# Float64 weights turned into float32: products on two engines, or moved bits and an int32 add on GpSimd, in another order of the first two units

## The chip, the cores and the metric

The kernel runs on one core of a Trainium2 chip. The core has five engines with a queue of instructions each: TensorE (PE in the profile, its weight loads PEld), VectorE (DVE), ScalarE (ACT), GpSimd (POOL) and SyncE (SP, which here issues transfers). The metric is the device time of one execution in microseconds.

## The reference

A gated linear attention over 768 steps, for 4 batches and 8 heads of 48 channels, and on its output a block of normalization and a two-layer MLP with a residual sum. `w_ch1` is 384 x 1536 and `w_ch2` 1536 x 384; both reach the kernel as float64, the other inputs as float32.

```python
f = 1.0 / (1.0 + np.exp(-f_logit))
for t in range(S):
    state = f[:, :, t, :, None] * state + np.einsum('bhd,bhe->bhde', k[:, :, t], v[:, :, t])
    y[:, :, t] = np.einsum('bhd,bhde->bhe', q[:, :, t], state)
x = y.transpose(0, 2, 1, 3).reshape(B, S, H * D)
mu, var = np.mean(x, -1, keepdims=True), np.var(x, -1, keepdims=True)
xn = (x - mu) / np.sqrt(var + 1e-06) * g_ln
out = x + np.maximum(xn @ w_ch1, 0.0) @ w_ch2
```

## The kernel before

The 768 steps are cut into twelve units of 64 steps of all four batches. A unit has an attention, written as a generator with stages, and an MLP with twelve parts. Each engine executes its instructions in the order in which the program writes them; that order is written out by hand at the end of the kernel (the calls of `do.attention`, `do.mlp` and `weights`), so an instruction that waits holds everything written behind it on its engine.

The stages of a unit's attention, with the tiles and lines that matter here:

- gates: PE transposes the raw `f` (L509), ACT makes the sigmoid `gates` (L542)
- after, upto: DVE's two scans over 1040 columns (L523, L535)
- k, q: PE transposes `k` and `q`, DVE multiplies them out of PSUM into `kh` and `qh` (L559); at the end of q DVE makes `kept`, the decayed state (L568)
- scores: PE multiplies the carried state (L579) and `ps` (L589)
- causal, kt, values: DVE masks the scores into `sc` (L593), PE transposes `kh` (L602), ACT copies that; PE makes `py` (L611), ACT copies it into `x` (L622)
- stats: DVE's statistics of `x` (L626, L627), and on GpSimd `rstd` by an add (L628) and a power (L629), both of two columns
- state: PE makes `pn` (L637), from which the new `state` is made (L642; by ACT in unit 0)
- norm, turn: DVE makes `xn` (L656); PE transposes it into `xp` (L666), and six products on ACT, each of which reads the tile `gain`, make `xt` (L668)

An MLP's first six parts make `ph` with w1 (L681: twelve matmuls as the profile counts them; one relu on ACT, L683). Its last six make `po` with w2 (L688: eight matmuls each, three parts for each half of the unit).

The weights come in twelve pieces of 128 x 768 numbers, six of w1 and then six of w2. Piece i of w1 is all that part i of `ph` needs, and piece i of w2 serves two of the twelve steps of a `po` sum, so that the third part of `po` is the first to need pieces five and six. `fetch` issues the transfer of the next piece from SP into `words`, of which there are three buffers. `split` and `join` make float32 of a piece: `split` (L464 to L472) takes exponent and fraction apart on DVE and turns each into a float32 factor on ACT, `join` (L481 to L485) adds the low word, puts in the sign and multiplies, on DVE. In the profile, names of pieces are cut to their columns (`w_0words` to `w_1280words` for w1, and `w_0` again for each piece of w2).

Unit 0's attention runs first, then unit 0's `ph` parts between unit 1's attention stages, each part behind its piece of w1; then unit 1's `ph` parts, beside which w2's pieces are made; then the `po` parts of units 0 and 1 beside unit 2's attention. From unit 2 on, each unit's MLP runs beside the next unit's attention. `load` issues a unit's four inputs, four transfers of 96 KB for each, from SP; unit 1's `f` is issued between the second and third piece, `gain` behind it.

Of the kernel before, what the change touches and what calls it, by code (L numbers as in the profile page):

```python
# [8 lines left out]
FP32 = mybir.dt.float32  # L9
I32 = mybir.dt.int32  # L10
U32 = mybir.dt.uint32
AF = mybir.ActivationFunctionType
ALU = mybir.AluOpType
# [290 lines left out]
def kernel(  # L304
# [19 lines left out]
    nc = tc.nc  # L324
    B, H, S, D = q.shape
    P = 128
# [12 lines left out]
    EPS = 1e-6  # L339
    LEAST = 1e-12  # L340
    PIECE = 768
    BIAS = 1023 - 127

    outer = ctx.enter_context(tc.tile_pool(name="outer", bufs=1))
    ident = outer.tile([P, P], FP32)
# [7 lines left out]
    consts = fast.enter_context(tc.tile_pool(name="consts", bufs=1))  # L353
    raws = fast.enter_context(tc.tile_pool(name="raws", bufs=3))
    stage = fast.enter_context(tc.tile_pool(name="stage", bufs=3))
# [22 lines left out]
    def load(n, name, engines=(nc.sync,)):  # L378
        if n >= NU:
            return  # L380
        if name == "v":
            vt = raws.tile([P, G, H, D], FP32, tag="rawv", name=f"v{n}")
            loaded[n, name] = vt
        else:
            loaded[n, name] = wide_heads[name, n % 2]
        src = {"f": f_logit, "k": k, "q": q, "v": v}[name]
        for b in range(B):
            engines[b % len(engines)].dma_start(  # L388
                out=loaded[n, name][(b % 2) * T:(b % 2 + 1) * T, b // 2, :, 0:D],
                in_=src[b, :, n * T:(n + 1) * T, :].rearrange("h p d -> p h d"))  # L390
# [15 lines left out]
    for b in range(2):  # L406
        nc.gpsimd.affine_select(out=causal[b * T:(b + 1) * T], in_=causal[b * T:(b + 1) * T],
                                compare_op=ALU.is_ge, fill=0.0, base=0, pattern=[[1, T]],
                                channel_multiplier=-1)
    bias = consts.tile([P, 1], FP32)  # L410
    nc.vector.memset(bias, float(-BIAS))
    full = consts.tile([P, 1], FP32)
    nc.vector.memset(full, 255.0)

    ends = consts.tile([P, NS, E1], FP32)
    nc.vector.memset(ends, 0.0)
# [1 line left out]
    starts, gates = [], []  # L418
# [8 lines left out]
    nc.vector.memset(least, 1.0)  # L427
    state = consts.tile([P, 2, GA, D], FP32)


    def pieces(dst, src, name, by_rows):
        rows, cols = dst.shape[1], dst.shape[2]
        sv = src.rearrange("(c p) f -> p c f", p=P)
        r, w = (PIECE // cols, cols) if by_rows else (rows, PIECE // rows)
        return [(f"{name}{i}_{j}", sv[:, i:i + r, j:j + w], dst[:, i:i + r, j:j + w], r, w)
                for i in range(0, rows, r) for j in range(0, cols, w)]
# [3 lines left out]
    fetched, opened = [], []  # L440

    def fetch():
        if not queue:
            return
        name, src, to, r, w = queue.pop(0)
        if not wide:
            nc.sync.dma_start(out=to, in_=src)
            return
        words = stage.tile([P, r, 2 * w], I32, tag="words", name=f"{name}words")
        nc.sync.dma_start(out=words, in_=src.bitcast(I32))  # L450
        fetched.append((name, words, to, r, w))

    def split():

        if not fetched:
            return
        name, words, to, r, w = fetched.pop(0)
        scale = stage.tile([P, r, w], I32, tag="scale", bufs=2, name=f"{name}scale")
        frac = stage.tile([P, r, w], FP32, tag="frac", bufs=2, name=f"{name}frac")
        wv = words.rearrange("p r (f two) -> p two r f", two=2)  # L460
        low, high = wv[:, 0].bitcast(U32), wv[:, 1]


        nc.vector.tensor_scalar(out=scale, in0=high, scalar1=20, scalar2=0x7FF,  # L464
                                op0=ALU.logical_shift_right, op1=ALU.bitwise_and)
        nc.vector.tensor_scalar(out=frac.bitcast(I32), in0=high, scalar1=0xFFFFF, scalar2=None,
                                op0=ALU.bitwise_and)
        nc.scalar.activation(out=frac, in_=frac.bitcast(I32), func=AF.Copy, bias=1.0,
                             scale=2.0 ** -20)
        nc.scalar.activation(out=scale, in_=scale, func=AF.Relu, bias=bias, scale=1.0)  # L470
        nc.scalar.activation(out=scale, in_=scale, func=AF.Relu, bias=full, scale=-1.0)  # L471
        nc.scalar.activation(out=scale, in_=scale, func=AF.Copy, bias=float(255 << 23),  # L472
                             scale=float(-(1 << 23)))
        opened.append((low, high, scale, frac, to))

    def join():

        if not opened:
            return
        low, high, scale, frac, to = opened.pop(0)  # L480
        nc.vector.scalar_tensor_tensor(out=frac, in0=low, scalar=2.0 ** -52, in1=frac,  # L481
                                       op0=ALU.mult, op1=ALU.add)
        nc.vector.scalar_tensor_tensor(out=scale, in0=high, scalar=-(1 << 31), in1=scale,  # L483
                                       op0=ALU.bitwise_and, op1=ALU.bitwise_or)
        nc.vector.tensor_tensor(out=to, in0=frac, in1=scale.bitcast(FP32), op=ALU.mult)  # L485

# [229 lines left out]

    do = Order()


    fetch()
    fetch()
    load(1, "f")
    nc.sync.dma_start(out=gain, in_=moe_g_ln.rearrange("(c p) -> p c", p=P))
    fetch()
    for name in "kqv":
        load(1, name)

    def weights(*steps):  # L730
        for step in steps:
            step()
            if step is join:
                fetch()

    do.attention(0, "gates", "after", "upto", "k", "q", "scores")
    weights(split)
    do.attention(0, "causal", "kt", "values")
    weights(join, split)
    do.attention(0, "stats", "state")  # L740
    do.attention(1, "gates")
    weights(join, split)
    do.attention(0, "norm", "turn")
    do.mlp(0)
    weights(join, split)
    do.mlp(0)
    for _ in range(3):
        weights(join, split)
        do.mlp(0)
    do.attention(1, "after", "upto", "k", "q")  # L750
    weights(join)
    do.mlp(0)
    do.attention(1, "scores")
    weights(split)
    do.attention(1, "causal", "kt", "values")
    weights(join, split)
    do.attention(1, "stats", "state")
    weights(join)
    do.attention(1, "norm", "turn")
    for part in range(6):  # L760
        do.mlp(1)
        weights(split, join)
        if part == 3:
            for name in "fkqv":
                load(2, name)
    assert not (queue or fetched or opened)
# [20 lines left out]
    for m in range(2, NU):  # L787
        n = m + 1
        for part in range(12):
# [19 lines left out]
            if n == NU and part == 2:  # L809
                worst = consts.tile([P, 1], FP32)  # L810
                nc.vector.tensor_reduce(out=worst, in_=least, axis=mybir.AxisListType.X,
                                        op=ALU.min)
# [6 lines left out]
                                        op0=ALU.is_lt)  # L819
# [36 lines left out]
```

## Time and profile before

| what | us |
|---|---|
| median of 3 runs | 546.14 (545.92 to 546.4) |
| the profiled execution | 545.63, of which its span 543.9 |
| PE busy in the span | 500.2 (92%) |
| PEld, DVE, ACT, POOL busy | 384.9, 212.1, 140.0, 16.4 |

The profile is of one execution; times in it run from the start of the span. Busy time of PE is no measure of its speed, since matmuls are pipelined. Where a row names a wait, it gives the idle time of the engine ahead of the instruction and what ended it.

### The profile page before, as it was taken

How to read it: one execution, taken by the hardware profiler on the slowest of the kernel's cores; microseconds unless marked ns; L12 is line 12 of the kernel's file. 1: busy time of each engine (PE TensorE's matmuls, PEld its weight loads, DVE VectorE, ACT ScalarE, POOL GpSimd, SP SyncE). 2: the span in 40 equal slices, each digit the busy share in tenths (PEclk: the TensorE clock that was granted, in tenths of full speed). 3: DMA queues.
4: the chain of work that ended last, by engine and by line, in shares of the span. 5: the costliest groups of instructions: out<-in, count | busy, mean ns of one | idle time of the engine just before them, and what ended most of it. 6: DMA issues, size and time to landing. Idle time of an engine off the chain costs nothing.

```text
span 543.9 us, 10888 instructions
## 1 busy us (share of the span) xinstructions
PE 500.2 (92%) x4841; PEld 384.9 (71%) x4841; DVE 212.1 (39%) x312; ACT 140.0 (26%) x267; POOL 16.4 (3%) x41
## 2 busy tenths in 40 slices
PE   4556468999999999999999999999999999999995
PEld 3545356767787786786786786786786786786873
DVE  7656883672253243243243243243242342341000
ACT  1656464601221221211211211211221220220210
POOL 3100000000000000000000000000000000000000
PEclk9969787999999999999999999999999999999999
DMA  7973138134150240340340240340330340000001
GB/s 137 230 214 116 58 118 155 20 75 88 39 93 2 57 90 2 60 86 2 63 85 1 60 88 6 67 75 10 65 74 13 63 72 16 16 1 16 16 2 33
DMA packets 109702, 33.82 MB, mean 62 GB/s; under 512 B 102736, under 2 KB 105808, under 8 KB 109648
## 3 DMA queue, kind: packets, MB, share of 16 engines
q1 hardware_dynamic: 108592, 32.85, 29.0%
q8 instruction: 40, 0.66, 0.5%
q10 hardware_dynamic: 1056, 0.20, 0.2%
q14 instruction: 14, 0.11, 0.1%
HBM read 28.31 MB, written 4.72 MB: 61 GB/s over the span
## 4 chain that ended last, share of the span: by engine, by line
PE 84%; DVE 6%; ACT 5%; SPq 2%; DMA 1%; issue 1%
PE po L688 35%; PE ph L681 33%; PE tr L509 5%; PE py L611 4%; PE py L579 2%; PE kp L602 2%; PE ps L589 2%; SPq L388 2%; PE pn L637 2%; DVE w L485 1%; PE xp L666 1%; DMA w_0words<-in_moe_w_ch_dram 1%; DVE w_0scale L483 1%; ACT w_0scale L471 1%; ACT w_0scale L472 0%
## 5 line engine op out<-in xcount | busy, mean ns | idle before, releaser
L681 PE MATMUL ph<-xt,w 128*128 128x256 f32 x864 | 200.9, 389 | 7.8 <-DVE w L485 4.6
L688 PE MATMUL po<-w,h 128*128 128x384 f32 x576 | 192.6, 488 | 0.0
L681 PEld LDWEIGHTS ph<-xt,w 128*128 128x128 f32 x864 | 166.7, 196 | 34.2 <-issue 4.1
L688 PEld LDWEIGHTS po<-w,h 128*128 128x128 f32 x576 | 106.8, 190 | 67.7
L683 ACT ACTIVATE h<-ph 128x512 f32<-128x512 f32 x72 | 42.7, 596 | 168.5 <-PE ph L681 168.5
L693 DVE TENSOR_TENSOR o<-x,po 128x384 f32<-128x384 f32 x24 | 13.3, 553 | 105.2 <-PE po L688 105.2
L523 DVE TENSOR_TENSOR_SCAN after<-gates,ends 128x1040 f32<-128x1040 f32 (+1 forms) x13 | 28.0, 2156 | 35.4 <-ACT gates L542 35.4
L668 ACT ACTIVATE xt<-xp,gain 128x128 f32<-128x128 f32 x72 | 19.9, 376 | 83.1 <-PE xp L666 83.1
L626 DVE BATCH_NORM_STATS2 stats<-x 128x6 f32<-128x384 f32 x24 | 13.0, 543 | 69.0 <-ACT x L622 69.0
L593 DVE TENSOR_TENSOR sc<-ps,causal 128x1024 f32<-128x1024 f32 x12 | 14.7, 1224 | 53.9 <-PE ps L589 53.9
L535 DVE TENSOR_TENSOR_SCAN upto<-gates,starts 128x1040 f32<-128x1040 f32 (+1 forms) x13 | 28.1, 2158 | 0.5
L611 PEld LDWEIGHTS py<-v,sc 64*64 64x64 f32 x768 | 23.3, 135 | 6.6 <-issue 5.5
L622 ACT COPY x<-py 128x384 f32<-128x384 f32 x24 | 10.3, 484 | 64.8 <-PE py L611 64.8
L611 PE MATMUL py<-v,sc 64*64 64x48 f32 x768 | 24.8, 219 | 0.5 <-DVE sc L593 0.5
L666 PE MATMUL xp<-ident,xn 128*128 128x128 f32 x72 | 11.2, 298 | 14.4 <-DVE xn L656 14.4
L559 DVE TENSOR_TENSOR qh<-tr,upto 128x512 f32<-128x512 f32 x24 | 15.5, 686 | 19.6 <-PE tr L509 19.6
L666 PEld LDWEIGHTS xp<-ident,xn 128*128 128x128 f32 x72 | 9.5, 154 | 17.9 <-issue 9.2
L604 ACT COPY kt<-kp 128x512 f32<-128x512 f32 x24 | 12.9, 587 | 35.2 <-PE kp L602 35.2
L509 PE MATMUL tr<-ident,qraw 128*128 128x128 f32 x96 | 14.3, 292 | 7.4 <-DVE kh L559 7.2
L509 PEld LDWEIGHTS tr<-ident,qraw 128*128 128x128 f32 x96 | 12.0, 150 | 9.6 <-DVE kh L559 7.4
L509 PE MATMUL tr<-ident,fraw 128*128 128x128 f32 x96 | 13.6, 286 | 5.0 <-DMA fraw<-in_f_logit_dram 5.0
L628 POOL TENSOR_SCALAR rstd<-mv 128x2 f32<-128x2 f32 x12 | 3.2, 270 | 481.0 <-DVE mv L627 481.0
(102 smaller groups left out, 318.8 us busy)
## 6 DMA issues: line engine op xcount, KB each, us to landing
w_0words<-in_moe_w_ch_dram SPq DMA_DIRECT2D x7, 768.0 KB, 4.4
kraw<-in_k_dram SPq DMA_DIRECT2D x48, 96.0 KB, 3.1
qraw<-in_q_dram SPq DMA_DIRECT2D x48, 96.0 KB, 3.1
v<-in_v_dram SPq DMA_DIRECT2D x48, 96.0 KB, 2.9
out_dram<-o SPq DMA_DIRECT2D x48, 96.0 KB, 2.2
fraw<-in_f_logit_dram SPq DMA_DIRECT2D x46, 96.0 KB, 3.0
w_256words<-in_moe_w_ch_dram SPq DMA_DIRECT2D x1, 768.0 KB, 6.8
w_512words<-in_moe_w_ch_dram SPq DMA_DIRECT2D x1, 768.0 KB, 7.0
```

The source lines that it names most:

```text
L509: nc.tensor.transpose(pt[:, a * P:(a + 1) * P], src[:, g, 2 * a:2 * a + 2].rearrange("p h e -> p (h e)"), ident)
L523: nc.vector.tensor_tensor_scan(out=after.rearrange(flat)[:, c0:c1][:, ::-1], data0=gt[:, c0 + 1:c1 + 1][:, ::-1], data1=ends.rearrange(fla ...
L535: nc.vector.tensor_tensor_scan(out=upto.rearrange(flat)[:, c0:c1], data0=gt[:, c0:c1], data1=st.rearrange(flat)[:, c0:c1], initial=0.0, op ...
L559: nc.vector.tensor_tensor(out=dst[:, segs], in0=pt, in1=by[:, segs, 1:E1], op=ALU.mult)
L593: nc.vector.tensor_tensor(out=sc.rearrange("s r e t -> s (r e) t"), in0=ps.rearrange("s r e t -> s (r e) t"), in1=causal.unsqueeze(1).broa ...
L611: nc.tensor.matmul(py[half(b), r, e * D:(e + 1) * D], lhsT=sc[half(b), r, e], rhs=vt[half(b), g, 2 * a + r], start=n == 0 and e == 0, stop ...
L666: nc.tensor.transpose(pt[:, m], xn[:, g, m * P:(m + 1) * P], ident)
L668: nc.scalar.mul(out=xt[:, m, g * P:(g + 1) * P], in_=pt[:, m], mul=gain[:, m:m + 1])
L681: nc.tensor.matmul(ph[:, j], lhsT=w1[:, m, (i + j) * P:(i + j + 1) * P], rhs=xt[:, m], start=m == 0, stop=m == KD - 1)
L683: nc.scalar.activation(out=h[:, i:i + 2], in_=ph, func=AF.Relu)
L688: nc.tensor.matmul(po, lhsT=h[:, i, g * P:(g + 1) * P], rhs=w2[:, i], start=i == 0, stop=i == KF - 1)
L693: nc.vector.tensor_tensor(out=o, in0=x[:, g], in1=po, op=ALU.add)
```

## The change

It exchanges the way a float32 is made, the order in which the first two units are written, and the order of some transfers.

`read` in place of `split`: ACT alone reads the words. The high word, taken as a float32 and multiplied by 2^-112, becomes `upper`; the low word, scaled by 2^-29 and rounded by adding and taking away 2^23, becomes the int32 `units`. The buffer of words is free then. `write` in place of `join`: DVE clamps `upper`, shifts its bits left by three and puts the sign in, and GpSimd adds `units` as int32 numbers and writes the weight. `fetch` follows each `read`, not each `join`. The two constants `bias` and `full` go.

In the order, unit 0's statistics, state, norm and turn come directly behind its values, with one piece written and another read between, and unit 1's stages are put between unit 0's `ph` parts. The loads of unit 1 are all issued ahead of `gain` and of w1's third piece. Unit 2's loads are issued one part later.

```diff
-    def split():
+    def read():
-        scale = stage.tile([P, r, w], I32, tag="scale", bufs=2, name=f"{name}scale")
-        frac = stage.tile([P, r, w], FP32, tag="frac", bufs=2, name=f"{name}frac")
+        upper = stage.tile([P, r, w], FP32, tag="upper", bufs=2, name=f"{name}upper")
+        units = stage.tile([P, r, w], FP32, tag="units", bufs=2, name=f"{name}units")
         wv = words.rearrange("p r (f two) -> p two r f", two=2)
-        low, high = wv[:, 0].bitcast(U32), wv[:, 1]
-        nc.vector.tensor_scalar(out=scale, in0=high, scalar1=20, scalar2=0x7FF,
-                                op0=ALU.logical_shift_right, op1=ALU.bitwise_and)
-        nc.vector.tensor_scalar(out=frac.bitcast(I32), in0=high, scalar1=0xFFFFF, scalar2=None,
-                                op0=ALU.bitwise_and)
-        nc.scalar.activation(out=frac, in_=frac.bitcast(I32), func=AF.Copy, bias=1.0,
-                             scale=2.0 ** -20)
-        nc.scalar.activation(out=scale, in_=scale, func=AF.Relu, bias=bias, scale=1.0)
-        nc.scalar.activation(out=scale, in_=scale, func=AF.Relu, bias=full, scale=-1.0)
-        nc.scalar.activation(out=scale, in_=scale, func=AF.Copy, bias=float(255 << 23),
-                             scale=float(-(1 << 23)))
+        low, high = wv[:, 0].bitcast(U32), wv[:, 1].bitcast(FP32)
+        nc.scalar.activation(out=upper, in_=high, func=AF.Copy, scale=2.0 ** -112)
+        nc.scalar.activation(out=units, in_=low, func=AF.Copy, bias=2.0 ** 23, scale=2.0 ** -29)
+        nc.scalar.activation(out=units.bitcast(I32), in_=units, func=AF.Copy, bias=-2.0 ** 23)
-    def join():
+    def write():
-        nc.vector.scalar_tensor_tensor(out=frac, in0=low, scalar=2.0 ** -52, in1=frac,
-                                       op0=ALU.mult, op1=ALU.add)
-        nc.vector.scalar_tensor_tensor(out=scale, in0=high, scalar=-(1 << 31), in1=scale,
+        body = stage.tile([P, r, w], FP32, tag="body", bufs=1, name=f"{name}body")
+        nc.vector.tensor_scalar(out=body, in0=upper, scalar1=-INF, scalar2=INF, op0=ALU.max,
+                                op1=ALU.min)
+        body, upper = body.bitcast(I32), upper.bitcast(I32)
+        nc.vector.tensor_scalar(out=body, in0=body, scalar1=3, scalar2=None,
+                                op0=ALU.logical_shift_left)
+        nc.vector.scalar_tensor_tensor(out=upper, in0=upper, scalar=-(1 << 31), in1=body,
                                        op0=ALU.bitwise_and, op1=ALU.bitwise_or)
-        nc.vector.tensor_tensor(out=to, in0=frac, in1=scale.bitcast(FP32), op=ALU.mult)
+        nc.gpsimd.tensor_tensor(out=to.bitcast(I32), in0=upper, in1=units, op=ALU.add)
...
     fetch()
     fetch()
-    load(1, "f")
+    for name in "fkqv":
+        load(1, name)
     nc.sync.dma_start(out=gain, in_=moe_g_ln.rearrange("(c p) -> p c", p=P))
     fetch()
-    for name in "kqv":
-        load(1, name)
...
     do.attention(0, "gates", "after", "upto", "k", "q", "scores")
-    weights(split)
+    piece(read)
     do.attention(0, "causal", "kt", "values")
-    weights(join, split)
-    do.attention(0, "stats", "state")
-    do.attention(1, "gates")
-    weights(join, split)
-    do.attention(0, "norm", "turn")
+    piece(write, read)
+    do.attention(0, "stats")
+    piece(write)
+    do.attention(0, "state", "norm", "turn")
+    do.attention(1, "gates", "after")
     do.mlp(0)
-    weights(join, split)
+    do.attention(1, "upto")
+    piece(read)
     do.mlp(0)
-    for _ in range(3):
-        weights(join, split)
-        do.mlp(0)
-    do.attention(1, "after", "upto", "k", "q")
-    weights(join)
+    do.attention(1, "k")
+    piece(write, read)
     do.mlp(0)
-    do.attention(1, "scores")
-    weights(split)
+    do.attention(1, "q", "scores")
+    piece(write, read)
     do.attention(1, "causal", "kt", "values")
-    weights(join, split)
-    do.attention(1, "stats", "state")
-    weights(join)
-    do.attention(1, "norm", "turn")
+    do.mlp(0)
+    piece(write, read)
+    do.attention(1, "stats", "state", "norm")
+    do.mlp(0)
+    piece(write, read)
+    do.attention(1, "turn")
+    do.mlp(0)
     for part in range(6):
         do.mlp(1)
-        weights(split, join)
-        if part == 3:
+        piece(write, read)
+        if part == 4:
             for name in "fkqv":
                 load(2, name)
```

## Rows read from the trace of the kernel before

**Rows 1.** The page: PE's busy tenths in 40 slices of the span.

```profile
PE   4556468999999999999999999999999999999995
```

**Rows 2.** Waits of PE, 0 to 104: us in total, times, longest.

```profile
PE xp L666 <- DVE xn L656: 14.4, 2, 7.2
...
PE tr L509 <- DVE kh L559: 7.2, 1, 7.2
```

**Rows 3.** Timeline, fourth piece of w1: start, us, engine, line, what.

```profile
35.20 0.55 DVE L464 TENSOR_SCALAR w_768scale<-w_768words 128x768 int32<-128x768 int32 x1
...
39.66 0.83 ACT L468 ACTIVATE w_768frac<-w_768frac 128x768 f32<-128x768 int32 x1
...
43.19 0.96 DVE L483 SCALAR_TENSOR_TENSOR w_768scale<-w_768words,w_768scale 128x768 int32<-128x768 int32 x1 [1.71 <-ACT w_768scale L472]
```

**Rows 4.** Timeline of PE, 33 to 104; in brackets the idle time before.

```profile
51.76 4.51 PE L681 MATMUL ph<-xt,w 128*128 128x256 f32 x12 [3.71 <-DVE w L485]
...
64.76 1.12 PE L509 MATMUL tr<-ident,qraw 128*128 128x128 f32 x4 [7.18 <-DVE kh L559]
...
69.98 1.15 PE L579 MATMUL py<-kept,qh 48*64 48x48 f32 x64
...
75.31 1.16 PE L637 MATMUL pn<-v,kt 64*64 64x48 f32 x64
...
85.82 17.58 PE L681 MATMUL ph<-xt,w 128*128 128x256 f32 x72 [0.59 <-ACT xt L668]
```

**Rows 5.** The chain that ended last: start, us, what.

```profile
34.38 4.76 PE ph L681 x12
...
141.24 2.58 PE po L688 x8
...
147.28 5.18 PE ph L681 x24
```

**Rows 6.** Timeline of DVE, 23 to 80.

```profile
24.54 0.93 DVE L481 SCALAR_TENSOR_TENSOR w_256frac<-w_256words,w_256frac 128x768 f32<-128x768 uint32 x1
...
29.66 0.87 DVE L656 TENSOR_SCALAR xn<-x,mv,rstd 128x384 f32<-128x384 f32 x2
...
58.95 2.32 DVE L523 TENSOR_TENSOR_SCAN after<-gates,ends 128x1040 f32<-128x1040 f32 x1
...
66.61 0.95 DVE L568 TENSOR_TENSOR kept<-state,total 128x768 f32<-128x768 f32 x1
...
78.97 0.92 DVE L642 TENSOR_TENSOR state<-kept,pn 128x768 f32<-128x768 f32 x1
```

**Rows 7.** Timeline of POOL, 0 to 80.

```profile
2.56 0.29 POOL masks.py:199 TENSOR_SCALAR_AFFINE_SELECT ident<-ident 128x128 f32<-128x128 f32 x1
...
24.72 0.83 POOL L628 TENSOR_SCALAR rstd<-mv 128x2 f32<-128x2 f32 x1 [19.25 <-DVE mv L627]
25.63 0.71 POOL L629 TENSOR_TENSOR rstd<-rstd,power 128x2 f32<-128x2 f32 x1
79.14 0.22 POOL L628 TENSOR_SCALAR rstd<-mv 128x2 f32<-128x2 f32 x1 [52.80 <-DVE mv L627]
```

**Rows 8.** Timeline of ACT, 14 to 45.

```profile
33.21 1.64 ACT L668 ACTIVATE xt<-xp,gain 128x128 f32<-128x128 f32 x6
```

**Rows 9.** Timeline of SP's issues, 10 to 35.

```profile
15.80 1.93 SPq L725 DMA_DIRECT2D gain<-in_moe_g_ln_dram  x1
...
18.31 3.68 SPq L388 DMA_DIRECT2D kraw<-in_k_dram  x4
...
26.40 2.67 SPq L388 DMA_DIRECT2D v<-in_v_dram  x4
```

**Rows 10.** DMA issues, 0 to 130: count, KB each, median us to landing.

```profile
v<-in_v_dram SPq DMA_DIRECT2D x16, 96.0 KB, 3.0
...
gain<-in_moe_g_ln_dram SPq DMA_DIRECT2D x1, 1.5 KB, 6.2
```

**Rows 11.** Windows: length, PE busy (x), PEclk, DMA share, GB/s.

```profile
51.70:56.20 4.50, 4.44 (x13) 0.62 0.53 171
```

More of the change, by code (lines that the diff above doesn't have):

```diff
@@ L341 @@
     PIECE = 768
-    BIAS = 1023 - 127
     outer = ctx.enter_context(tc.tile_pool(name="outer", bufs=1))
@@ L409 @@
                                 channel_multiplier=-1)
[L410 to L413, printed above, removed]
     ends = consts.tile([P, NS, E1], FP32)
@@ L428 @@
     state = consts.tile([P, 2, GA, D], FP32)
+    INF = 2.0 ** -96 * 1.875
     def pieces(dst, src, name, by_rows):
@@ L471, in split @@
-        nc.scalar.activation(out=scale, in_=scale, func=AF.Relu, bias=full, scale=-1.0)
-        nc.scalar.activation(out=scale, in_=scale, func=AF.Copy, bias=float(255 << 23),
-                             scale=float(-(1 << 23)))
-        opened.append((low, high, scale, frac, to))
-    def join():
+        low, high = wv[:, 0].bitcast(U32), wv[:, 1].bitcast(FP32)
+        nc.scalar.activation(out=upper, in_=high, func=AF.Copy, scale=2.0 ** -112)
+        nc.scalar.activation(out=units, in_=low, func=AF.Copy, bias=2.0 ** 23, scale=2.0 ** -29)
@@ L478, in join @@
+        nc.scalar.activation(out=units.bitcast(I32), in_=units, func=AF.Copy, bias=-2.0 ** 23)
+        opened.append((upper, units.bitcast(I32), to, name, r, w))
+    def write():
         if not opened:
             return
-        low, high, scale, frac, to = opened.pop(0)
-        nc.vector.scalar_tensor_tensor(out=frac, in0=low, scalar=2.0 ** -52, in1=frac,
-                                       op0=ALU.mult, op1=ALU.add)
-        nc.vector.scalar_tensor_tensor(out=scale, in0=high, scalar=-(1 << 31), in1=scale,
+        upper, units, to, name, r, w = opened.pop(0)
+        body = stage.tile([P, r, w], FP32, tag="body", bufs=1, name=f"{name}body")
[5 more added lines that the diff above has]
+        nc.vector.scalar_tensor_tensor(out=upper, in0=upper, scalar=-(1 << 31), in1=body,
@@ L719, with piece @@
     do = Order()
+    def piece(*steps):
+        for step in steps:
+            step()
+            if step is read:
+                fetch()
     fetch()
     fetch()
-    load(1, "f")
+    for name in "fkqv":
+        load(1, name)
     nc.sync.dma_start(out=gain, in_=moe_g_ln.rearrange("(c p) -> p c", p=P))
     fetch()
-    for name in "kqv":
-        load(1, name)
[L730 to L734, printed above, removed]
     do.attention(0, "gates", "after", "upto", "k", "q", "scores")
-    weights(split)
+    piece(read)
     do.attention(0, "causal", "kt", "values")
-    weights(join, split)
-    do.attention(0, "stats", "state")
-    do.attention(1, "gates")
-    weights(join, split)
-    do.attention(0, "norm", "turn")
+    piece(write, read)
[3 more added lines that the diff above has]
+    do.attention(1, "gates", "after")
     do.mlp(0)
-    weights(join, split)
+    do.attention(1, "upto")
+    piece(read)
     do.mlp(0)
-    for _ in range(3):
-        weights(join, split)
-        do.mlp(0)
-    do.attention(1, "after", "upto", "k", "q")
-    weights(join)
+    do.attention(1, "k")
+    piece(write, read)
     do.mlp(0)
-    do.attention(1, "scores")
-    weights(split)
+    do.attention(1, "q", "scores")
+    piece(write, read)
     do.attention(1, "causal", "kt", "values")
-    weights(join, split)
-    do.attention(1, "stats", "state")
-    weights(join)
-    do.attention(1, "norm", "turn")
+    do.mlp(0)
[5 more added lines that the diff above has]
+    do.mlp(0)
     for part in range(6):
         do.mlp(1)
-        weights(split, join)
-        if part == 3:
+        piece(write, read)
+        if part == 4:
             for name in "fkqv":
```

## The prediction

> **What bounds the kernel now.** I read the page first. In its forty slices [rows 1] TensorE (PE) is at 9 from the eighth slice on, and only before that, up to about 86 us, are there gaps. Later the chain that ended last is one matmul behind another [rows 5], so a change to weight preparation can win only ahead of 86 us. There PE's table of waits [rows 2] names the cause: 14.4 us for `xn`, 7.2 for `kh`. These waits are for VectorE (DVE), and the timeline shows why DVE is late: its queue runs in the written order, and a piece of weights in front of `xn` or of unit 1's scans holds it while ScalarE (ACT) makes its four products [rows 3]. When unit 1's MLP begins at 85.82, PE has just idled, and those 72 matmuls take 17.58 us [rows 4], against 5.18 for 24, or 2.59 a part of twelve, in the steady stretch [rows 5]. So the question is when unit 1's MLP can begin; behind it the order on PE is the same, part for part, and the time saved there is saved at the end. I call that moment S.
>
> **The price of a piece.** Before, ACT runs four products of 0.83 and a little more, and DVE two at 0.55 and three at 0.96, 3.98 in all [rows 3]. After, ACT runs three, of which the last needs the second: about 2.45 us, 0.84 to `upper`. DVE runs clamp and shift at 0.55 and the sign at 0.96: 2.1 with gaps. All three exist before in these sizes. No row shows ACT reading every second word; DVE does it at no extra price [rows 3, 6], so I add nothing for ACT. GpSimd (POOL) gets twelve int32 adds of 128x768, and no row has such an add. The nearest that reads and writes a tile is the 128x128 select at 0.29 [rows 7]; six times that is 1.74. Below, a bound is the 0.22 of a two-column add; above, twice 1.74, about 3.5, if the second input costs as much as the first. With the 0.71 of the power on top of 1.74 [rows 7] it would be 2.45. I take A = 1.74, nearest to the select, and 1.9 with its two handovers.
>
> **The start.** The two memsets that go lay beside idle time. Unit 0's `xn` no longer stands behind the second piece's products and the third's masks. Its statistics are done no later than before, by 24.5 where `frac` starts behind them [rows 6]; 0.22 and 0.71 for `rstd`, some 0.9 for `xn` and a microsecond of transposes would let the first `xt` product start at 27.5, and being 1.2 ahead of the first `ph` [rows 5, 8], let unit 0's MLP begin by 28.7; I take 28. But each `xt` product reads `gain`, and its transfer is moved past twelve loads on SP's queue. Before, it is issued at 15.80, takes SP 1.93, and lands 6.2 after issue [rows 9, 10]. After, the twelve go first. They took SP 10.8 before (18.31 to 29.07, with w1's third piece in front of them), and at v's rate of 0.67 they would take 8.1 [rows 9]. So gain is issued between 23.9 and 26.6, I take 25.2. From issue it takes between 4.2 (its 1.93 and what v needs beyond its own issue, 2.3) and 6.2, I take 5.2. It lands between 28.1 and 32.8, at 30.4 by the middle. That is a wait which takes the place of the one removed: behind the `xt` products on ACT stand unit 1's gates, and behind those the scans. The MLP begins at 30.4 + 1.2 = 31.6. w1's third piece is moved past the same loads and lands a few microseconds behind gain; ACT wants it at 36.7, so I count nothing for it; late, it costs what it exceeds that by, less some 2.
>
> **From there to S**, along PE, the weights and DVE. The first part at the low clock, as the twelve matmuls behind a wait of 3.71 took 4.51 at a granted clock of 0.62, that is, for the most part at 1.2 and not at 2.4 GHz [rows 4, 11]: 36.1. The second at 2.59: 38.7. k's transposes and `kh`, by q's transposes and products, which took 1.8 from 64.76 to `kept` at 66.61 [rows 4, 6]: 40.5. (The scans, two at 2.32 and half a microsecond [rows 6], start at 33.2 behind gates and are done by 38.4, in time.) Only now, by the written order, does DVE write the third piece, though its `upper` was ready: 2.1, and the add 1.9: 44.5. PE has then idled almost 5 us, so the third part is slow again, 4.5: 49.0. q's transposes to the end of `kept`, 2.8 (64.76 to 67.56): 51.8. Then PE's run from the carried state to unit 1's last `pn`, 6.5 (69.98 to 76.47) [rows 4], with the fourth part now inside it, 2.6: 60.9. Pieces four and five are written and added under this; on POOL `rstd` now stands behind them, but the fifth's add ends some 2 us before `state` is there. `state` 0.92 and `xn` 0.87 [rows 6]: 62.7. The fifth part of `ph` runs beside them. The sixth piece is written behind `xn`, 2.1, and added, 1.9: 66.7; unit 1's transposes and `xt` products fit below that. The sixth part, 2.6: S = 69.3. That is 16.5 before 85.82. PE will have idled only about 1.5 by then, so I let unit 1's six parts run at the full clock, 15.5 in place of 17.58: another 2.0. Together 18.5.
>
> **w2.** Beside unit 1's MLP each part lets one piece through. The second w2 piece is read when the first relu is done, S + 3.2; `upper` is there at S + 4.05, DVE has done at 6.15, and POOL adds from 6.25. The last piece, four later, is wanted by the third part of `po`: six parts, two `po` parts at 2.58 [rows 5] and a microsecond of transposes, S + 21.8. If write and add can run side by side, ACT sets the pace at 3.0 (relu 0.6, read 2.4): S + 18.2 + A, 20, in time. If not, a piece takes 2.2 + A: the last is ready at S + 15.05 + 5A, at 23.8, 2.0 late.
>
> Unit 2's loads stand on SP behind the last fetch, some 5 us into this stretch, and are first wanted 15 later.
>
> Which is it? POOL's two-column add took 0.83 at 24.72, when DVE was in a two-input operation from 24.54 to 25.47; it ended 0.08 after that [rows 6, 7]. Its second case, at 79.14 beside `state`, of whose inputs one lies in PSUM, took 0.22. I take this for a lock between POOL and DVE operations that read SBUF twice, with one reserve: the slow case is also POOL's first of its kind. The Trainium skill (SBUF — State Buffer, Who interferes with whom) speaks against this change: a GpSimd instruction that reads SBUF and a VectorE one with two SBUF inputs, or in a two-port mode, exclude each other for whole instructions. The row of 24.72 agrees; by the rule the sum has the 2.0, without it not. With the lock the gain is 18.5 - 2.0 = 16.5.
>
> **The sum** against the profiled execution (545.63; 543.9 of span and 1.7 around it): 529.1. The median of runs is 0.5 higher, so 529.5 is what I expect to be measured. At this kernel's spread of some 0.2%, or 1 us, that is far from no change.
>
> **Rivals.** *No lock, or an add short enough* (under 1.35, where 15.05 + 5A fits into 21.8): 527.5. For it: 0.83 may be a first call. Against: it ended with DVE's operation. Chance 0.2. *Gain is in time* and `rstd` sets the start: ph 3.6 earlier, 526. For it: only 1.5 KB. Against: 6.2 before, and a long queue ahead. Chance 0.12. *A longer add*, 2.45: two on the path to S and the w2 row, so 7 us for each microsecond of A, 5 us: 534.5. Chance 0.14. *Slower*: the same slope cancels all of 16.5 where A passes 1.74 + 16.5/7 = 4.1; GpSimd is then the bound for the weights, with PE waiting at every w1 piece and at w2's last. At 4.5 the time is 549. For it: POOL takes 0.71 for two columns of a power. Against: 0.29 for 128 columns of a select, and 4.1 is above twice that rate. Chance 0.04. *The rest* (the third words late, ACT slower on strided words at up to 0.6 more an instruction, the clock up or down at another part, 2 us each): 0.05.
>
> The Trainium skill (GPSIMD Engine Reference, Performance versus the Vector engine) gives 4497 ns for a two-input add of 2048 columns; in proportion that would be an estimated 1.69, and a sum 0.4 below mine.
>
> **How the numbers follow.** The forecast with lock and late gain holds 0.45. From 522 (no lock, gain in time, one part more at the full clock) to 537 (A near 2.8, or a further late transfer with A at 2.4) lies all but some 0.17. Faster by over 0.2%: all but the slow add and a bad remainder, 0.94; within 0.2%: 0.02; slower: 0.04.
>
> **What would show it.** Right: the first `xt` waits for gain's transfer, near 30; `ph`'s third and sixth parts wait for POOL's add; unit 1's MLP begins near 69 and runs its parts at 2.6; POOL's adds take about 1.7 and start or end with DVE's operations; a wait of 2 us before unit 0's third `po` part. Wrong: adds of 3 us or more, gates of unit 1 right behind its transposes, new waits of PE after 92 us, or a first part of unit 1's MLP at the low clock (2 us more).

## The result and the profile after

The changed kernel takes 530.13 us (529.68 to 532.93, 4 runs) against 546.27 of the kernel before beside it: a ratio of 0.9713, 95% interval 0.9677 to 0.9749, so 2.5 to 3.2% faster. The forecast was 529.5 in 522 to 537. The profiled execution took 529.85, its span 528.0, 15.9 less than before.

The page of the changed kernel, PE's busy tenths in forty slices, answers to [rows 1]: PE is at 9 from the sixth slice on, where it was from the eighth.

```profile
PE   4686799999999999999999999999999999999995
```

The waits of PE over the whole span (us in total, times, longest) answer to [rows 2]. Of the 21.6 us of waits for `xn` and `kh` 4.9 are left, and GpSimd's adds have come in: 7.4 at `ph`, where PE waited 4.6 for DVE's weights before, and 0.9 at `po`.

```profile
PE ph L678 <- POOL w L482: 7.4, 2, 4.9
...
PE xp L663 <- DVE xn L653: 4.9, 2, 3.5
...
PE po L685 <- POOL w L482: 0.9, 1, 0.9
```

The timeline of PE, from unit 0's first `ph` to the third part of `po`, answers to [rows 4]:

```profile
29.99 7.09 PE L678 MATMUL ph<-xt,w 128*128 128x256 f32 x24 [0.33 <-ACT xt L665]
...
42.90 4.88 PE L678 MATMUL ph<-xt,w 128*128 128x256 f32 x12 [4.94 <-POOL w L482]
...
50.55 1.15 PE L576 MATMUL py<-kept,qh 48*64 48x48 f32 x64 [1.90 <-DVE kept L565]
...
66.36 20.08 PE L678 MATMUL ph<-xt,w 128*128 128x256 f32 x84 [2.43 <-POOL w L482]
86.28 5.32 PE L685 MATMUL po<-w,h 128*128 128x384 f32 x16
...
92.32 1.46 PE L685 MATMUL po<-w,h 128*128 128x384 f32 x4
94.70 4.14 PE L685 MATMUL po<-w,h 128*128 128x384 f32 x12 [0.92 <-POOL w L482]
```

The row of 66.36 holds unit 0's sixth part and unit 1's six. ACT's relu on the first of them starts at 70.80 (timeline of ACT), so S is 70.75, and unit 1's six parts take 15.5 to 86.28. Before, `po` began at 103.23 (timeline of PE, before):

```profile
70.80 0.60 ACT L680 ACTIVATE h<-ph 128x512 f32<-128x512 f32 x1 [2.90 <-PE ph L678]
```

```profile
103.23 5.32 PE L688 MATMUL po<-w,h 128*128 128x384 f32 x16
```

The 16.95 gained there less the 0.92 of waiting at 94.70 are 16.0, within 0.1 the whole difference of the spans: behind that the kernels run alike.

ACT, SP and POOL in the timeline of the changed kernel; the wait for `gain`, which is issued at 26.23, answers to [rows 8, 9], the adds to [rows 7]:

```profile
26.23 0.62 SPq L728 DMA_DIRECT2D gain<-in_moe_g_ln_dram  x1
...
28.71 1.66 ACT L665 ACTIVATE xt<-xp,gain 128x128 f32<-128x128 f32 x6 [3.96 <-DMA gain<-in_moe_g_ln_dram]
...
41.04 1.80 POOL L482 TENSOR_TENSOR w<-w_512upper,w_512units 128x768 int32<-128x768 int32 x1 [14.26 <-DVE w_512upper L480]
...
81.38 2.19 POOL L482 TENSOR_TENSOR w<-w_0upper,w_0units 128x768 int32<-128x768 int32 x1 [2.22 <-DVE w_0upper L480]
...
85.20 2.19 POOL L482 TENSOR_TENSOR w<-w_0upper,w_0units 128x768 int32<-128x768 int32 x1 [1.63 <-DVE w_0upper L480]
```

DVE in the same timeline: `xn`, the shift alone (39.34) and beside an add (81.94), and unit 2's first scan. [rows 6] has `xn` and a scan without an add.

```profile
24.65 2.35 DVE L653 TENSOR_SCALAR xn<-x,mv,rstd 128x384 f32<-128x384 f32 x2
...
39.34 0.56 DVE L478 TENSOR_SCALAR w_512body<-w_512body 128x768 int32<-128x768 int32 x1
...
81.94 2.06 DVE L478 TENSOR_SCALAR w_0body<-w_0body 128x768 int32<-128x768 int32 x1
...
93.20 3.62 DVE L520 TENSOR_TENSOR_SCAN after<-gates,ends 128x1040 f32<-128x1040 f32 x1 [0.50 <-ACT gates L539]
```

An add alone takes 1.80. Where it meets one of these DVE operations, one of the two stands, and the profile shows the standing inside its time: the shift takes 2.06 in place of 0.56, the scan 3.62 in place of 2.32. The adds of w2 follow each other every 3.82 us (81.38 to 85.20), which is about the 2.0 of the write and the 1.8 of the add one after the other.

### The profile page after: what moved, and what is told of

Read it like the earlier page. It is cut to its first block, busy times and chain, and to the rows that moved or that the text cites. A ratio compares the mean times of both kernels' runs of the same rounds, so it can differ in the third digit from the quotient of the medians.

```text
span 528.0 us, 10900 instructions
## 1 busy us (share of the span) xinstructions
PE 498.3 (94%) x4841; PEld 383.8 (73%) x4841; DVE 202.0 (38%) x286; ACT 129.1 (24%) x255; POOL 39.2 (7%) x53
## 4 chain that ended last, share of the span: by engine, by line
PE 86%; DVE 5%; SPq 5%; POOL 1%; ACT 1%; issue 1%; DMA 0%; DVEq 0%; POOLq 0%; ACTq 0%
PE po L685 34%; PE ph L678 34%; PE tr L506 5%; SPq L387 4%; PE py L608 4%; PE py L576 2%; PE ps L586 2%; PE kp L599 2%; PE pn L634 2%; DVE w_0body L478 1%; PE xp L663 1%; POOL w L482 1%; DVE w_0upper L480 1%; DVE w_0body L475 1%; DMA gain<-in_moe_g_ln_dram 0%
## 5 line engine op out<-in xcount | busy, mean ns | idle before, releaser
L520 DVE TENSOR_TENSOR_SCAN after<-gates,ends 128x1040 f32<-128x1040 f32 (+1 forms) x13 | 29.3, 2256 | 39.6 <-ACT gates L539 39.6
L608 PEld LDWEIGHTS py<-v,sc 64*64 64x64 f32 x768 | 24.4, 139 | 6.7 <-issue 5.8
L608 PE MATMUL py<-v,sc 64*64 64x48 f32 x768 | 26.0, 223 | 0.6 <-DVE sc L590 0.3
L506 PEld LDWEIGHTS tr<-ident,fraw 128*128 128x128 f32 x96 | 12.5, 155 | 6.5 <-POOL causal L406 4.5
L586 PE MATMUL ps<-qh,kh 48*64 48x64 f32 x768 | 14.4, 227 | 2.7 <-DVE qh L556 2.7
L482 POOL TENSOR_TENSOR w<-w_0upper,w_0units 128x768 int32<-128x768 int32 x7 | 13.8, 1974 | 30.3 <-DVE w_0upper L480 30.3
L556 DVE TENSOR_TENSOR kh<-tr,after 128x512 f32<-128x512 f32 x24 | 15.2, 674 | 1.0 <-PE tr L506 1.0
```

The costliest lines, as they stand in the source:

```text
L482: nc.gpsimd.tensor_tensor(out=to.bitcast(I32), in0=upper, in1=units, op=ALU.add)
L506: nc.tensor.transpose(pt[:, a * P:(a + 1) * P], src[:, g, 2 * a:2 * a + 2].rearrange("p h e -> p (h e)"), ident)
L520: nc.vector.tensor_tensor_scan(out=after.rearrange(flat)[:, c0:c1][:, ::-1], data0=gt[:, c0 + 1:c1 + 1][:, ::-1], data1=ends.rearrange(fla ...
L556: nc.vector.tensor_tensor(out=dst[:, segs], in0=pt, in1=by[:, segs, 1:E1], op=ALU.mult)
L586: nc.tensor.matmul(ps[half(b), r, e], lhsT=kh[head_rows(r), seg], rhs=qh[head_rows(r), seg], start=True, stop=True)
L608: nc.tensor.matmul(py[half(b), r, e * D:(e + 1) * D], lhsT=sc[half(b), r, e], rhs=vt[half(b), g, 2 * a + r], start=n == 0 and e == 0, stop ...
```

## The experiments

Each was timed beside the kernel before; ratios are to that. Order alone, conversion alone, no add and the first run of gain early were on one chip; add twice, or on DVE, the first run of the third piece written ahead, and the three together on a second; the changed kernel again, the two repeats beside it and the busy wait on a third.

**Which half of the change pays.** The new order with the old products, and the moved bits and add in the old order. The edits are the two halves of the diff; what they come to:

```diff
 # order alone
-    piece(read) ... piece(write, read)     # moved bits, int32 add
+    piece(split) ... piece(join, split)    # masks and products, in the new order
 # conversion alone
-    weights(split) ... weights(join, split)
+    weights(read) ... weights(write, read) # in the old order, old loads and fetches
```

> The new order of the first two units with the old products (two masks and three two-input operations on VectorE, four products on ScalarE). Theory A, the cheaper piece is what pays and the order only makes use of it: xn still stands behind the second piece's products, so unit 0's first ph begins near 32 us and unit 1's MLP near 72, and then the w2 pieces, six at some 6.5 us each in a row of masks, products and joins, hold po: the last is ready 35 us after unit 1's MLP begins and is wanted after 22. In sum 540 to 548 us, no gain to speak of. Theory B, the order pays by itself (unit 0's chain ahead of the pieces): 532 to 536.

Measured 547.92, ratio 1.003 (1.0017 to 1.0042): 0.3% slower than before.

> The moved bits and GpSimd's add in the old order of stages, loads and fetches. Theory A, the cheaper piece is what pays: the pieces still stand in front of xn, but each takes ScalarE 2.6 in place of 3.5 us and VectorE 2.1 in place of 4.0, and three w2 pieces are done ahead of unit 1's MLP, which begins at 66 to 72: 526 to 533 us, within 4 us of the changed kernel. Theory B, the order pays: 538 to 544, since xn and unit 1's scans still stand behind the pieces.

Measured 531.96, ratio 0.974 (0.9719 to 0.9761). Theory A holds and B falls: the cheaper piece by itself brings 14 of the 16 us, and the new order by itself loses 1.5. With the old products PE waits in the new order for DVE and, behind it, at `po` (waits of PE, order alone; lines are that kernel's):

```profile
PE ph L688 <- DVE w L492: 7.8, 2, 5.7
PE po L695 <- DVE w L492: 7.0, 3, 4.0
PE xp L673 <- DVE xn L663: 5.9, 1, 5.9
```

With the conversion alone unit 1's MLP begins at 71.88, and `po` waits for nothing, since three w2 pieces are made ahead (timeline of PE, conversion alone):

```profile
68.64 0.90 PE L662 MATMUL xp<-ident,xn 128*128 128x128 f32 x3 [4.48 <-DVE xn L652]
...
71.88 16.99 PE L677 MATMUL ph<-xt,w 128*128 128x256 f32 x72 [0.46 <-ACT xt L664]
88.71 5.32 PE L684 MATMUL po<-w,h 128*128 128x384 f32 x16
```

The order is not worthless, though. It holds the late transfer of `gain` too, and with that transfer early the new order with the new conversion takes 527.35 on this chip (below), 4.6 less than the conversion alone.

**What the add costs.** Without it, and with it done twice. The first also leaves out ACT's two products on the low words, and DVE's sign operation writes the weight:

```diff
 # no add: the low words are left out
-        nc.scalar.activation(out=units, in_=low, func=AF.Copy, bias=2.0 ** 23, scale=2.0 ** -29)
-        nc.scalar.activation(out=units.bitcast(I32), in_=units, func=AF.Copy, bias=-2.0 ** 23)
...
-        nc.vector.scalar_tensor_tensor(out=upper, in0=upper, scalar=-(1 << 31), in1=body,
+        nc.vector.scalar_tensor_tensor(out=to.bitcast(I32), in0=upper, scalar=-(1 << 31), in1=body,
                                        op0=ALU.bitwise_and, op1=ALU.bitwise_or)
-        nc.gpsimd.tensor_tensor(out=to.bitcast(I32), in0=upper, in1=units, op=ALU.add)
 # add twice
         nc.gpsimd.tensor_tensor(out=to.bitcast(I32), in0=upper, in1=units, op=ALU.add)
+        nc.gpsimd.tensor_tensor(out=to.bitcast(I32), in0=upper, in1=units, op=ALU.add)
```

> The changed kernel without the low words: ScalarE makes only upper, VectorE writes the weight, GpSimd adds nothing, so the three last bits of each weight are left out. If the add and its exclusion of VectorE cost what the trace shows, this gives back 2 us at the third part of ph, 2 at the sixth and with that the low clock there (another 1.8), and 0.9 at po: 522 to 525 us. If the adds lie beside other work, under 2 us: 528 to 530.

Measured 524.01, ratio 0.96 (0.9575 to 0.9624), 6 below the changed kernel. The timeline of PE, no add, has the third part and the row with the sixth:

```profile
42.09 4.36 PE L674 MATMUL ph<-xt,w 128*128 128x256 f32 x12 [3.09 <-DVE w L477]
...
62.60 18.37 PE L674 MATMUL ph<-xt,w 128*128 128x256 f32 x84 [0.57 <-DVE w L477]
```

The waits there are 3.09 from 4.94 and 0.57 from 2.43, the seven parts run at the full clock (18.37 in place of 20.08), and `po` does not wait: 6.3 in all. The run takes add and products away together; that it is the add follows from the changed kernel's timeline, where the products of the third and sixth pieces end at 37.60 and 62.51, ahead of the sign operations (40.90 and 64.35) that the adds also need.

> The changed kernel with each of GpSimd's adds done twice, so that a piece costs 3.65 there in place of 1.8. By the prediction's slope (two adds on the way to unit 1's MLP, then five in a row of w2 with write and add excluding each other: 7 us for each microsecond) 13 us more: 540 to 547 us, with a wait of 8 us or more at po. If write and add of neighbouring pieces could overlap, only the two on the way would count: 533 to 536.

Measured 548.16, ratio 1.003 (1.0011 to 1.005): 1.9 us of add more a piece cost 17 to 18, so 9 to 10 for each microsecond, not the 7 forecast; the time lies above the range given, and all of the gain is gone at an add of 3.7. The waits of PE, add twice, show where: three at `ph`, not two, since `rstd` and the fifth piece now stand behind the doubled adds, and three at `po`.

```profile
PE ph L679 <- POOL w L483: 12.8, 3, 6.8
PE po L686 <- POOL w L483: 8.8, 3, 3.6
```

**The low bits without GpSimd.** ACT makes them in one product, rounded down and not to nearest, and DVE shifts and sets them in with an or:

```diff
-        nc.scalar.activation(out=units, in_=low, func=AF.Copy, bias=2.0 ** 23, scale=2.0 ** -29)
-        nc.scalar.activation(out=units.bitcast(I32), in_=units, func=AF.Copy, bias=-2.0 ** 23)
+        nc.scalar.activation(out=units.bitcast(I32), in_=low, func=AF.Copy, bias=-0.49999,
+                             scale=2.0 ** -29)
...
+        nc.vector.scalar_tensor_tensor(out=upper, in0=upper, scalar=-(1 << 31), in1=units,
+                                       op0=ALU.bitwise_and, op1=ALU.bitwise_or)
-        nc.gpsimd.tensor_tensor(out=to.bitcast(I32), in0=upper, in1=units, op=ALU.add)
+        nc.vector.scalar_tensor_tensor(out=to.bitcast(I32), in0=body, scalar=3, in1=upper,
+                                       op0=ALU.logical_shift_left, op1=ALU.bitwise_or)
```

> The changed kernel without GpSimd: ScalarE makes the low bits in one product (rounded down, not to nearest), and VectorE shifts and sets them in by bitwise or, one clamp and two two-input operations of 0.96, 2.5 us a piece in place of 2.1 and 1.9 on GpSimd. By the path 1.4 less at each of the third and sixth parts, the full clock at the sixth, no wait at po: 523.5 to 526, some 1 above the kernel without the low words (524.0). If instead VectorE's longer work is the bound: 529 or more.

Measured 526.71, ratio 0.9656 (0.9628 to 0.9685): 3 to 4 below the changed kernel, a little above the range given.

**The late transfer of gain.**

```diff
+    nc.sync.dma_start(out=gain, in_=moe_g_ln.rearrange("(c p) -> p c", p=P))
     for name in "fkqv":
         load(1, name)
-    nc.sync.dma_start(out=gain, in_=moe_g_ln.rearrange("(c p) -> p c", p=P))
```

> The changed kernel with gain's transfer ahead of unit 1's loads. By the prediction's reading the wait for gain (3.96 us on ScalarE, until 28.7) sets unit 0's first ph, and without it ph would begin 1.5 to 2 us earlier: 528 to 528.5 us. By the trace of the changed kernel it would be covered: the second half of xn is held by GpSimd's add until 27.0, and the transposes of unit 1's f end on TensorE at 29.7, so ph begins 0.3 earlier at most: 529.5 to 530.2, the same.

Measured 527.35, ratio 0.9654 (0.9633 to 0.9674): below both ranges, further from that of the second reading. The four executions lay within 0.5 us. To be sure of the chip, the changed kernel and this one ran again side by side:

> The changed kernel once more, on the chip of the next three, so that their differences of 2 or 3 us are read on one chip: 529 to 531 us if chips do not matter here; 527 to 528 if the differences read so far were the chip's.

Measured 530.78 (529.02 to 533.39), ratio 0.972 (0.9695 to 0.9745).

> The changed kernel with gain's transfer ahead of unit 1's loads, beside the changed kernel on one chip. If the first reading (527.35) was gain's: 2 to 3 us below the changed kernel, though ph begins only 0.3 earlier, the rest from a TensorE clock that rises earlier. If it was the chip or the moment at which the clock falls: within 1 us of it.

Measured 527.49 (527.27 to 528.06), ratio 0.9658 (0.9642 to 0.9675). So 3.3 us are gain's, a little more than the 2 to 3 given. The first two parts of `ph` in the timeline of PE, the changed kernel again, and the windows of a microsecond behind (length, PE busy (x), PEclk, DMA share, GB/s):

```profile
29.58 8.20 PE L678 MATMUL ph<-xt,w 128*128 128x256 f32 x24 [0.68 <-ACT xt L665]
```

```profile
33.00:34.00 1.00, 1.00 (x4) 0.50 1.08 416
34.00:35.00 1.00, 1.00 (x4) 0.50 0.49 178
```

and with gain early:

```profile
28.68 6.87 PE L678 MATMUL ph<-xt,w 128*128 128x256 f32 x24
```

```profile
31.00:32.00 1.00, 1.00 (x5) 0.62 1.07 404
32.00:33.00 1.00, 1.00 (x6) 1.00 1.04 393
```

`ph` begins 0.9 earlier, but its second part ends 2.2 earlier (35.55 against 37.78): with no gap between the transposes of `f` and `ph`, the granted clock is back at 2.4 GHz by 32, and at 1.2 GHz until 35 with the gap. Seven traces of the changed kernel and of variants that are alike up to here but for `gain` agree: in the three without that gap the second part ends at 35.51 to 35.55, in the four with a gap of 0.33 to 1.15 at 37.08 to 38.18. One of the three has `gain` late (the first run of the next experiment), so a late `gain` does not bring the gap in each execution.

**Two waits further on.** The third piece written ahead of unit 1's k stage, twice, and PE kept busy in the wait ahead of the sixth part:

```diff
+    piece(write)
     do.attention(1, "k")
-    piece(write, read)
+    piece(read)
```

> The changed kernel with the third piece written ahead of unit 1's k stage on VectorE. Its upper is there at 35.9 and VectorE is free at 36.6, but waits for k's transposes first. If this order is what makes the 4.9 us wait of the third part of ph, the wait falls to 2.7 and the time to 527 to 528.5. If kh, now later, is wanted as early, nothing moves: 530.

Measured 527.12, ratio 0.9667 (0.964 to 0.9694). The time is in the range, but its trace has the wait at 3.91, not 2.7, and is the one above in which the second part ends at 35.51: part of its gain is not the third piece's.

> The changed kernel with the third piece written ahead of unit 1's k stage, beside the changed kernel on one chip. By the wait that it shortens (4.9 to 3.9 in its first trace) 1 us below the changed kernel; by the earlier rise of the clock seen there too, 2.5 to 3.

Measured 527.03 (525.77 to 527.59), ratio 0.9648 (0.9629 to 0.9667), beside 530.78: 3.7 less, more than either figure given. The timeline of PE in this second trace:

```profile
40.85 5.49 PE L678 MATMUL ph<-xt,w 128*128 128x256 f32 x12 [2.81 <-POOL w L482]
...
65.88 18.40 PE L678 MATMUL ph<-xt,w 128*128 128x256 f32 x84 [2.43 <-POOL w L482]
```

The third part's wait is 2.81, from 4.94, which is 2.1 of it; the six parts of unit 1 and the one ahead of them also ran at the full clock here, 18.40 in place of 20.08, though the wait ahead of them was the same 2.43. Five other traces have that wait (2.42 or 2.43), and all five have 20.08.

```diff
     do.attention(1, "turn")
+    busy = one_bank("busy")
+    for _ in range(16):
+        nc.tensor.transpose(busy[:, 0:P], ident, ident)
     do.mlp(0)
```

> The changed kernel with sixteen transposes of the identity, which nobody reads, in TensorE's 2.4 us of waiting ahead of the sixth part of ph. If it is the idle time there that brings the low clock (twelve matmuls in 4.4 in place of 2.6): 1.5 to 2 us below the changed kernel. If the clock falls anyway, or the transposes hold up the part: the same or up to 0.5 above.

Measured 531.71 (527.35 to 532.08), ratio 0.9724 (0.9695 to 0.9752): no gain in time. The timeline of PE, busy wait, has the seven parts at the full clock, as the first reading had it:

```profile
67.47 1.91 PE L757 MATMUL busy<-ident 128*128 128x128 f32 x16
70.07 18.40 PE L678 MATMUL ph<-xt,w 128*128 128x256 f32 x84 [0.69 <-POOL w L482]
```

But this execution had lost as much before: from the carried state to the fourth part is 8.1 us (52.14 to 60.26), with the granted clock at 0.50 from 53 to 59, and in the changed kernel again 6.7, so that its `po` begins at 88.30, that of the changed kernel again at 88.20. So PE at work in the wait went with the full clock behind it, as in the trace above a wait without work did; what decides is not shown.

**Together.** Or on DVE, gain early, and the third piece ahead of k:

> The low bits set in on VectorE, gain's transfer ahead of unit 1's loads, and the third piece written ahead of unit 1's k stage. If the three are apart on the path, 2.5 and 2 less than with the first alone: 519 to 522 us. If the clock gives part of it back (a shorter wait, but from an earlier start): 522 to 525.

Measured 519.91 (517.78 to 520.83), ratio 0.9533 (0.9507 to 0.9559), the fastest of all: 10 us below the changed kernel. Unit 0's first `ph` begins at 27.83 and the sixth part at 57.25 (timeline of PE, all three):

```profile
27.83 6.25 PE L677 MATMUL ph<-xt,w 128*128 128x256 f32 x24
...
36.63 2.83 PE L677 MATMUL ph<-xt,w 128*128 128x256 f32 x12 [1.69 <-ACT w_768units L466]
...
57.25 18.37 PE L677 MATMUL ph<-xt,w 128*128 128x256 f32 x84 [1.03 <-DVE w L480]
```

## Why the prediction was right

By its steps, forecast and then measured:

| step | forecast | changed kernel |
|---|---|---|
| a piece on DVE / the add | 2.1 / 1.74 | 2.1 / 1.80 |
| gain lands | 30.4 | 28.7 |
| unit 0's first `ph` | 31.6 | 29.99 |
| first two parts | 7.1 | 7.09 |
| their end to the third part | 5.8 | 5.8 |
| third part | 4.5 | 4.88 |
| q's transposes to `kept` | 2.8 | 2.9 |
| carried state to `pn`, with a part | 9.1 | 9.9 |
| `state`, `xn`, the sixth piece | 5.8 | 5.9 |
| sixth part | 2.6 | 4.4 |
| S | 69.3 | 70.75 |
| unit 1's six parts | 15.5 | 15.5 |
| wait at `po` | 2.0 | 0.92 |
| gain of the span | 16.5 | 15.9 |

The mechanism was right: the waits that the forecast names are there, for the engines that it names. That the gain came within 0.6 is in part luck, since terms that were off by 0.8 to 1.8 nearly cancel. Gain landed 2.4 after its issue and not 5.2: at 26.23 SP needed 0.62 for it, where it had needed 1.93 at 15.80. The stretch from the carried state to `pn` took 0.8 more. The sixth part was put at 2.6, which is the full clock, and PE's idle time by then at about 1.5; it idled 2.43 and the part ran at 1.2 GHz, 1.8 more (windows of PE, changed kernel):

```profile
69.00:70.00 1.00, 1.00 (x4) 0.50 0.22 81
```

And the w2 wait was counted to the start of the third `po` part, which is four matmuls of 0.36 before the last piece is wanted (row of 92.32): 1.46 of the 2.0 was not there, and small shifts brought 0.4 back. The add's 1.74, six times a select with one input, met 1.80, and no row of the prediction assured that. The column is one execution: the first two parts that fit to 0.01 here took 8.20 in another.

The lock between POOL and DVE, which the prediction read from one row against a reserve, is shown by the times of shift and scan, by the pace of 3.82, and by the adds done twice, where a w2 piece takes 5.2 to 5.5 (starts of its first adds, 84.75 to 106.26) though the two adds alone are 3.65. The Trainium skill (SBUF — State Buffer, Who interferes with whom) is borne out for the shift and the scan. What the prediction did not see is that the second piece's add also holds `xn`, below. That gain sets the start was right as well (3.96 of waiting), and its price, 3.6 by the prediction, is 3.3 by the pair of runs. But that agreement is luck: the prediction had `ph` 3.6 earlier, and with gain early it begins only 0.9 earlier, since `xn` stands behind the add and the transposes of unit 1's `f` stand ahead of `ph` on PE. The second part ends 2.2 earlier in the pair of traces, the rest of that through the clock, which the prediction did not say.

What the prediction left apart was which half of the change earns the gain. It told the waits as a matter of the order; the runs say that the order alone earns nothing, because each piece then still takes DVE and ACT in turn for 6.5 us, and that with the cheaper conversion it saves at most 1 to 2 us (531.96 against 530.13 and 530.78, intervals that overlap), but 4.6 once gain is early. The slope for a longer add was too flat, 7 where the doubled add gave 9 to 10: doubled, the adds also hold up `rstd` and the fifth part, which did not wait for them before.

Open is how much of the differences of 1 to 2 us is the moment at which the clock falls: executions of the changed kernel on one chip spread over 4 us, and neither the run that kept PE busy nor the traces with the same wait told.

## What to carry to other kernels

When work moves to an engine that seemed idle, price what that engine shuts out as well: without the low words and their adds of 1.8 us the kernel was 6 us faster here, and with the low bits set by DVE alone 3 to 4. When transfers are put in another order, follow the smallest one too: 1.5 KB behind twelve loads cost 3.3 us. And ahead of a reordering, test the two halves of the change alone, since the sum along the path can come out right without saying which half pays.

## What the runs showed of the hardware that was not expected

- `xn`, with one tile as input and two columns of scalars, was held by the add (24.88 to 26.79): the pair took 2.35 us in place of 0.87.
- An issue by SP of the same 1.5 KB took 1.93 us at 15.80 before and 0.62 at 26.23 after, and it landed 6.2 and 2.4 us later.
- ACT's copies took 0.91 us for 768 numbers at every second word (L465), 0.84 for dense ones (L467).
- The granted clock falls and rises at other moments from run to run of one kernel: its first two parts of `ph` took 7.09 us in one execution and 8.20 in another.
